# The opening of layer one: norm of tile 1 ahead of tile 2's statistics, tile 2's load ahead of the second weight half, rsqrt steps spread thinner on ScalarE

## Chip, cores, metric

One core of a Trainium2 chip. The metric is the device time of one execution in microseconds (us), lower is better. "Span" is the profile's first to last instruction of one profiled execution; in the runs that have both it is some 1.7 us shorter than the time (1301.6 and 1303.29 for the kernel before). A "slow run" is one in the upper tail of its kernel's runs.

## The reference

Two layers, each a local dilated attention (A) and an MLP over tokens (B), all with a layer norm ahead; 2048 tokens, width 1024, 32 heads, bf16.

```python
x = A_x
x = x + _A_ref(_layernorm(x, axis=-1), A_wqkv, A_wo)   # the change lies in the first microseconds of this line
x = x + _B_ref(_layernorm(x, axis=-1), B_w1, B_b1, B_w2, B_b2)
x = x + _A_ref(_layernorm(x, axis=-1), A_wqkv, A_wo)
x = x + _B_ref(_layernorm(x, axis=-1), B_w1, B_b1, B_w2, B_b2)
```

What matters: the first thing to do is a layer norm of x (16 tiles of 128 tokens) and the V projection of it (two column halves `n` per tile, so 32 units of eight matmuls of 128x512).

## The kernel before

`start_up` writes the instruction order of each engine by hand. For tile `k`: `S_` are two half statistics on VectorE, `A_` aggregates them to mean and variance, `R_` is the rsqrt (a Ln and an Exp on ScalarE), `N_` the norm on VectorE. Tiles 0 to 4 are transposed on TensorE (`tr`) and copied by ScalarE to `hT` in two halves (`C_`); tiles 5 to 15 go through a DMA transpose (`T_`). `V_(k, n, ..)` are the matmuls of one unit, `E_(k, n)` evicts its PSUM tile `m` (two buffers) on ScalarE. `x_load` and `w_load` are loads, all issued by SyncE.

```python
wm = m_tile()
for _ in range(14):                      # dummy matmuls, called "warm" in the profile
    chain_("PE", lambda: nc.tensor.matmul(wm[:], lhsT=warm[:, 0:P], rhs=warm[:], start=True, stop=True))
# ... cut
chain_("SP", x_load, 0, halves)
chain_("SP", x_load, 1)
chain_("SP", w_load, 0, 0)
chain_("SP", w_load, 0, 1)
chain_("SP", x_load, 2)
chain_("SP", x_load, 3)
chain_("SP", w_load, 1, 0)
chain_("SP", w_load, 1, 1)
for k in range(4, NT):
    chain_("SP", x_load, k)
# ... cut
pe = [(tr, 0), (V_, 0, 0, lo4), (tr, 1), (V_, 0, 0, hi4), (V_, 1, 0, lo4), (tr, 2), (V_, 1, 0, hi4),
      (V_, 2, 0, a8), (V_, 0, 1, a8), (tr, 3), (V_, 1, 1, a8), (V_, 2, 1, a8), (tr, 4)]
pe += [(V_, k, n, a8) for k in range(3, NT) for n in range(NDC)]
act = [(R_, 0), (C_, 0), (R_, 1), (C_, 1), (R_, 2), (E_, 0, 0), (C_, 2), (R_, 3), (E_, 1, 0), (R_, 4),
       (E_, 2, 0), (C_, 3), (E_, 0, 1), (R_, 5), (E_, 1, 1), (R_, 6), (C_, 4), (E_, 2, 1), (R_, 7)]
es = [(E_, k, n) for k in range(3, NT) for n in range(NDC)]
for j, e in enumerate(es):
    act.append(e)
    if j + 8 < NT:
        act.append((R_, j + 8))
dve = [(S_, 0, 0), (S_, 0, 1), (A_, 0)]
for k in range(NT):
    nx = k + 1 < NT
    if nx:
        dve.append((S_, k + 1, 0))
    dve.append((N_, k, halves if k == 0 else whole))
    if nx:
        dve += [(S_, k + 1, 1), (A_, k + 1)]
```

The softmax here doesn't subtract the row's maximum and nothing guards it: scores larger than these inputs give would overflow.

## Time and profile before

| | before |
|---|---|
| time, median of 3 (range) | 1304.42 us (1303.2 to 1306.94) |
| span of the profiled execution | 1301.6 us |
| TensorE busy | 98% |
| transposes of tiles 0, 1, 2 start | 6.18, 10.44, 13.23 us |
| unit (3,0) starts | 22.44 us |
| evictions of `m`, 26 to 40 us | 1.99 us apart |

The page of the kernel before; the last line is the chain of work that ended last, by engine.

```profile
span 1301.6 us, 20885 instructions
...
PE 1279.8 (98%) x9240; PEld 581.9 (45%) x9398; DVE 392.8 (30%) x654; ACT 385.1 (30%) x628; POOL 1.7 (0%) x11
...
PE 94%; DVE 3%; issue 1%; ACT 1%; DMA 0%; SPq 0%; another core or an unknown queue 0%
```

TensorE bounds the kernel nearly throughout, so a change of the opening can win only what TensorE loses there. Its timeline (start us, duration us, engine, line, operation, output<-input, count, and in brackets the idle time before and what ended it):

```profile
6.18 0.71 PE L244 MATMUL s<-ident,x 128*128 128x128 bf16 x8
7.57 1.04 PE L257 MATMUL m<-wv,hT 128*128 128x512 bf16 x4 [0.68 <-ACT hT L250]
10.44 0.62 PE L244 MATMUL s<-ident,x 128*128 128x128 bf16 x8 [1.84 <-DVE x L188]
10.90 1.89 PE L257 MATMUL m<-wv,hT 128*128 128x512 bf16 x8
13.23 0.62 PE L244 MATMUL s<-ident,x 128*128 128x128 bf16 x8 [0.45 <-DVE x L188]
13.91 4.26 PE L257 MATMUL m<-wv,hT 128*128 128x512 bf16 x19
...
22.44 39.74 PE L257 MATMUL m<-wv,hT 128*128 128x512 bf16 x173
...
68.70 7.07 PE L351 MATMUL m<-hT,wqk 128*128 128x512 bf16 x32
```

There is one gap of about 2 us ahead of tile 1's transposes (10.44) and a smaller one ahead of tile 2's (13.23); from 13.9 to 22.4 us no further one shows. (The last line, the first q/k matmul, is from a later window.) The chain of waits of the first 15 us (start us, us, what) tells where the first gap comes from:

```profile
3.21 6.00 DMA x<-in_A_x_dram
...
9.24 0.04 DVE bn L226
...
9.85 0.54 DVE x L188
...
10.44 0.63 PE s L244 x8
```

Tile 2's load is issued at 3.21 and lands at 9.2. VectorE waits for it, does the first half of tile 2's statistics, and only then the norm of tile 1 (9.85), which TensorE needs. VectorE's own timeline has the wait, 1.96 us:

```profile
9.24 0.69 DVE L226 BATCH_NORM_STATS2 bn<-x 128x6 f32<-128x512 bf16 x1 [1.96 <-DMA x<-in_A_x_dram]
9.85 0.53 DVE L188 TENSOR_SCALAR x<-x,mv,rs 128x1024 bf16<-128x1024 bf16 x1
```

Tile 1's own scale was there at 8.43.

ScalarE's timeline between 26 and 44 us shows the second loss:

```profile
26.09 0.29 ACT L174 ACTIVATE ln<-mv,eps 128x1 f32<-128x1 f32 x1 [0.98 <-DVE mv L230]
26.42 0.20 ACT L175 ACTIVATE rs<-ln 128x1 f32<-128x1 f32 x1
26.53 0.57 ACT L263 CAST v<-m 128x512 bf16<-128x512 f32 x1
...
28.52 0.57 ACT L263 CAST v<-m 128x512 bf16<-128x512 f32 x1
...
43.00 0.59 ACT L263 CAST v<-m 128x512 bf16<-128x512 f32 x1 [1.40 <-PE m L257]
44.73 0.59 ACT L263 CAST v<-m 128x512 bf16<-128x512 f32 x1 [1.14 <-PE m L257]
```

Every eviction (CAST `v<-m`) stands behind a Ln/Exp pair, which waits about 0.98 us for VectorE's mean and variance, so evictions come at VectorE's 1.99 us, not at TensorE's 1.73 (43.00 to 44.73). TensorE has two `m` buffers and is slowed down to that.

### The profile page before, as it was taken

To read this page: it belongs to the slowest core of one execution; us is meant where nothing else is said; L and a number is where in the kernel's file an instruction comes from. 1 tells how busy PE (TensorE), PEld (TensorE's weight loads), DVE (VectorE), ACT (ScalarE), POOL (GpSimd) and SP (SyncE) were. 2 spreads that over 40 slices of the span, in tenths; PEclk is the share of its full clock that TensorE was granted. 3 is DMA by queue.
4 is the path that set the end of the run, shared out by engine and by line. 5 is a ranking of instruction groups with operands and counts; after the bars stand their busy time and mean duration, and the time that the engine had idled before them with its cause. 6 is when DMAs were issued, how large, how long until landed. Compare 5 with 4: busy or idle time off the path is not lost.

```text
span 1301.6 us, 20885 instructions
## 1 busy us (share of the span) xinstructions
PE 1279.8 (98%) x9240; PEld 581.9 (45%) x9398; DVE 392.8 (30%) x654; ACT 385.1 (30%) x628; POOL 1.7 (0%) x11
## 2 busy tenths in 40 slices
PE   8999999999999999999999999999999999999998
PEld 3444444444444444444444444444444444444443
DVE  7346667820000013232300566688000000111111
ACT  5356776531111110000023667765211111000000
POOL 0000000000000000000000000000000000000000
PEclk9999999999999999999999999999999999999999
DMA  7621113452222236455532100144422222334320
GB/s 235 129 66 34 35 34 98 148 153 82 81 65 84 65 88 159 120 151 152 130 81 57 42 19 19 34 136 156 138 65 81 81 59 76 106 105 136 115 91 33
DMA packets 195818, 121.69 MB, mean 93 GB/s; under 512 B 37904, under 2 KB 177424, under 8 KB 195728
## 3 DMA queue, kind: packets, MB, share of 16 engines
q1 hardware_dynamic: 195728, 120.36, 32.5%
q8 instruction: 73, 1.20, 0.4%
q14 instruction: 17, 0.14, 0.0%
HBM read 96.48 MB, written 16.78 MB: 87 GB/s over the span
## 4 chain that ended last, share of the span: by engine, by line
PE 94%; DVE 3%; issue 1%; ACT 1%; DMA 0%; SPq 0%; another core or an unknown queue 0%
PE m L351 17%; PE s L514 15%; PE s L471 15%; PE acc L471 7%; PE m L471 7%; PE m L514 7%; PE acc L514 7%; PE m L444 7%; PE m L336 4%; PE m L257 2%; PE acc L405 1%; PE s L377 1%; PE acc L409 1%; DVE xn L446 1%; DVE x L188 0%
## 5 line engine op out<-in xcount | busy, mean ns | idle before, releaser
L514 PEld LDWEIGHTS <-w 128*128 128x128 bf16 x1792 | 175.3, 98 | 211.4
L471 PEld LDWEIGHTS <-w 128*128 128x128 bf16 x1792 | 175.3, 98 | 211.4
L351 PE MATMUL m<-hT,wqk 128*128 128x512 bf16 x963 | 231.0, 380 | 7.9 <-issue 7.0
L471 PE MATMUL s<-h,w 128*128 128x512 bf16 x878 | 201.2, 379 | 0.8
L514 PE MATMUL s<-g,w 128*128 128x512 bf16 x884 | 199.3, 379 | 0.7
L517 DVE SCALAR_TENSOR_TENSOR xo<-s,b_sb,xs 128x512 bf16<-128x512 f32 x32 | 24.0, 750 | 540.7 <-PE s L514 530.2
L351 PEld LDWEIGHTS <-wqk 128*128 128x128 bf16 x1024 | 90.5, 98 | 108.7 <-issue 12.9
L386 DVE TENSOR_TENSOR Pm<-pc,band 64x1152 bf16<-64x1152 bf16 x128 | 96.3, 752 | 65.2 <-ACT pc L381 63.2
L444 PE MATMUL m<-wo,oT 128*128 128x512 bf16 x498 | 111.5, 379 | 0.9
L381 ACT ACTIVATE pc<-s,shift 128x576 bf16<-128x576 f32 x128 | 87.8, 737 | 59.9 <-PE s L377 59.9
L471 PE MATMUL acc<-h,w 128*128 128x512 bf16 x440 | 103.1, 379 | 0.5
L514 PE MATMUL acc<-g,w 128*128 128x512 bf16 x436 | 99.7, 379 | 0.5
L471 PE MATMUL m<-h,w 128*128 128x512 bf16 x438 | 98.5, 379 | 0.5
L514 PE MATMUL m<-g,w 128*128 128x512 bf16 x436 | 98.3, 379 | 0.6
L174 ACT ACTIVATE ln<-mv,eps 128x1 f32<-128x1 f32 x64 | 18.9, 296 | 234.5 <-DVE mv L182 222.2
L478 ACT ACTIVATE g<-s,b_sb 128x1024 bf16<-128x1024 f32 x28 | 31.2, 1114 | 166.9 <-PE s L471 155.2
L444 PEld LDWEIGHTS <-oT 128*128 128x128 bf16 x512 | 49.4, 98 | 59.7 <-issue 1.3
L257 PE MATMUL m<-wv,hT 128*128 128x512 bf16 x250 | 56.6, 379 | 1.5 <-ACT hT L250 0.7
L423 DVE TENSOR_TENSOR oT<-acc,rd 128x512 bf16<-128x512 f32 x64 | 44.0, 687 | 39.6 <-ACT rd L421 39.6
L336 PE MATMUL m<-wv,hT 128*128 128x512 bf16 x251 | 55.2, 379 | 0.3
L446 DVE TENSOR_TENSOR xn<-m,xr 128x512 bf16<-128x512 f32 x64 | 44.0, 687 | 8.0 <-PE m L444 6.6
L357 DVE CAST qT<-m 128x512 bf16<-128x512 f32 x32 | 21.8, 681 | 80.8 <-PE m L351 80.8
(59 smaller groups left out, 627.0 us busy)
## 6 DMA issues: line engine op xcount, KB each, us to landing
w<-in_B_w_dram SPq DMA_DIRECT2D x56, 512.0 KB, 3.8
w<-in_B_w_dram SPq DMA_DIRECT2D x64, 448.0 KB, 4.6
wqk<-in_A_wqkv_dram SPq DMA_DIRECT2D x16, 512.0 KB, 5.9
xa<-xn SPq DMA_DIRECT2D x32, 256.0 KB, 2.0
xs<-xa SPq DMA_DIRECT2D x32, 256.0 KB, 3.2
wv<-in_A_wqkv_dram SPq DMA_DIRECT2D x8, 512.0 KB, 5.3
wo<-in_A_wo_dram SPq DMA_DIRECT2D x8, 512.0 KB, 5.0
xr<-in_A_x_dram SPq DMA_DIRECT2D x16, 256.0 KB, 2.9
```

The lines of the kernel that those rows point to most:

```text
L257: r = nc.tensor.matmul(pss_[k, n][:], lhsT=hT[:, kt, cols(*order[k])], rhs=wv[n][kt // 4][:, kt % 4, :], start=(kt == 0), stop=(kt == KD - 1))
L336: nc.tensor.matmul(ps[:], lhsT=hT[:, kt, cols(c, i)], rhs=wv[n][kt // 4][:, kt % 4, :], start=(kt == 0), stop=(kt == KD - 1))
L351: mm = nc.tensor.matmul(ps[:], lhsT=wts[part][:, kt, (g % 2) * P:(g % 2 + 1) * P], rhs=hT[:, kt, lo:lo + 512], start=(kt == 0), stop=(kt = ...
L381: nc.scalar.activation(out=pc[:, 2 * n:2 * n + 2].rearrange("p h t k -> p h (t k)"), in_=ss[n][:, :, 0:HB * HW], func=ACT.Exp, scale=scale ...
L386: nc.vector.tensor_tensor(out=pm[rp, :, b * HB:(b + 1) * HB, r * HK:r * HK + HW], in0=pc[rp], in1=mk, op=ALU.mult)
L423: nc.vector.tensor_tensor(out=oT[g][:, lo:lo + hb * P], in0=acc[:, 0, :], in1=rd[:], op=ALU.mult)
L444: mm = nc.tensor.matmul(ps[:], lhsT=oT[g][:, cols(c, i)], rhs=wo[n][g // 4][:, g % 4, :], start=(g == 0), stop=(g == NG - 1))
L446: nc.vector.tensor_tensor(out=xn[:, xs_], in0=ps[:], in1=xr[:, xs_], op=ALU.add)
L471: nc.tensor.matmul(pairs[fl][0][dc], lhsT=wt[c][:, i, fl * P:(fl + 1) * P], rhs=h2[c][i][:, dc * 512:(dc + 1) * 512], start=(k == 0), stop ...
L478: nc.scalar.activation(out=g[fb][:, fl, :].rearrange("p (n d) -> p n d", n=2), in_=t[:], func=ACT.Gelu_apprx_tanh, bias=b1_sb[:, ft:ft + 1])
L514: nc.tensor.matmul(aps[dc], lhsT=w2t[ft // HF][:, ft % HF, c::DIL], rhs=g[ft // GF][:, ft % GF, dc * 512:(dc + 1) * 512], start=(ft == 0), ...
L517: nc.vector.scalar_tensor_tensor(out=xo[:, dc * 512:(dc + 1) * 512], in0=aps[dc], scalar=b2_sb[:, i, c:c + 1], in1=xs[:, dc * 512:(dc + 1) ...
```

## The change

The intent: take away both losses by order alone. Tile 1's norm goes ahead of tile 2's statistics, tile 2's load ahead of the second weight half, rsqrt 1 between the two copies of tile 0, and the later rsqrt steps go three to four evictions instead of one to one. ScalarE's order for tiles 2 to 6 moves a little as well.

```diff
-        def C_(k):
-            for hf in range(2):
-                ks = slice(hf * KD // 2, (hf + 1) * KD // 2)
-                r = nc.scalar.copy(out=hT[:, ks, cols(*order[k])], in_=tps[k][:, ks, :])
-            return r
+        def C_(k, hf):
+            ks = slice(hf * KD // 2, (hf + 1) * KD // 2)
+            return nc.scalar.copy(out=hT[:, ks, cols(*order[k])], in_=tps[k][:, ks, :])
@@
         chain_("SP", w_load, 0, 0)
+        chain_("SP", x_load, 2)
         chain_("SP", w_load, 0, 1)
-        chain_("SP", x_load, 2)
         chain_("SP", x_load, 3)
@@
-        act = [(R_, 0), (C_, 0), (R_, 1), (C_, 1), (R_, 2), (E_, 0, 0), (C_, 2), (R_, 3), (E_, 1, 0), (R_, 4),
-               (E_, 2, 0), (C_, 3), (E_, 0, 1), (R_, 5), (E_, 1, 1), (R_, 6), (C_, 4), (E_, 2, 1), (R_, 7)]
+        act = [(R_, 0), (C_, 0, 0), (R_, 1), (C_, 0, 1), (C_, 1, 0), (C_, 1, 1), (R_, 2), (E_, 0, 0), (C_, 2, 0), (C_, 2, 1),
+               (E_, 1, 0), (R_, 3), (E_, 2, 0), (R_, 4), (E_, 0, 1), (C_, 3, 0), (C_, 3, 1), (R_, 5), (E_, 1, 1), (R_, 6),
+               (E_, 2, 1), (C_, 4, 0), (C_, 4, 1)]
         es = [(E_, k, n) for k in range(3, NT) for n in range(NDC)]
+        rs = [(R_, k) for k in range(7, NT)]
         for j, e in enumerate(es):
             act.append(e)
-            if j + 8 < NT:
-                act.append((R_, j + 8))
-        dve = [(S_, 0, 0), (S_, 0, 1), (A_, 0)]
-        for k in range(NT):
+            if rs and j % 4 != 3:
+                act.append(rs.pop(0))
+        dve = [(S_, 0, 0), (S_, 0, 1), (A_, 0), (S_, 1, 0), (N_, 0, halves), (S_, 1, 1), (A_, 1), (N_, 1, whole),
+               (S_, 2, 0), (S_, 2, 1), (A_, 2)]
+        for k in range(2, NT):
... (the norm's line in this loop, and the bookkeeping of what must be built before what: cut)
```

More of the change, by code (lines that the diff above doesn't have):

```diff
@@ L301, in start_up @@
                 dve.append((S_, k + 1, 0))
-            dve.append((N_, k, halves if k == 0 else whole))
+            dve.append((N_, k, whole))
             if nx:
@@ L308, in start_up @@
         qs = {"PE": pe, "ACT": act, "DVE": dve, "SP": sp}
-        need = {cast_biases: lambda: (load_biases,) in done, R_: lambda k: k in mvs, N_: lambda k, h: k in rss, tr: lambda k: (N_, k) in done, C_: lambda k: k in tps,
-                V_: lambda k, n, kts: ((C_, k) in done or (T_, k) in done), E_: lambda k, n: (V_, k, n) in done,
+        need = {cast_biases: lambda: (load_biases,) in done, R_: lambda k: k in mvs, N_: lambda k, h: k in rss, tr: lambda k: (N_, k) in done, C_: lambda k, hf: k in tps,
+                V_: lambda k, n, kts: ((C_, k, 1 if kts[-1] == KD - 1 else 0) in done or (T_, k) in done), E_: lambda k, n: (V_, k, n) in done,
                 T_: lambda k: (N_, k) in done}
@@ L321, in start_up @@
                     else:
-                        done.add((f, *args[:1]))
+                        done.add((f, *(args if f is C_ else args[:1])))
     def load_wv():
```

## The prediction

> **What bounds the kernel.** The page shows TensorE busy 98% of 1301.6 us and 94% of the chain that ended last. The change touches only the opening of layer one, so it can win back only TensorE time lost in the first 42 us. The V projection there is 32 units of eight matmuls; one takes 1.727 us where nothing holds it (spacing of the ScalarE evictions of `m` after 43 us, timeline). Everything later just shifts.
>
> **Where TensorE loses now.** (1) Its timeline shows gaps before the transposes of tiles 1 and 2 at 10.44 and 13.23 us. By the chain of waits, tile 1's norm (9.85) stands on VectorE behind the first half of tile 2's statistics (9.24), which waited 1.96 us for tile 2's load, issued at 3.21 behind both 512 KB weight halves, landing 6.0 us later. Tile 1's scale was ready at 8.43, itself behind both copies of tile 0 on ScalarE. (2) From 22 to 40.5 us each eviction stands behind an rsqrt pair that waits about 0.99 us for VectorE's mean/variance: evictions come every 1.99 us instead of 1.727. Unit (3,0) starts at 22.44; freely run, the 11th unit from there would end at 22.44 + 11 x 1.727 = 41.43 and be evicted at 41.6. It was evicted at 43.00: 1.4 us lost (two `m` buffers absorb the rest).
>
> **What the change does.** No work is added or removed; order changes.
> - Norm 1 goes ahead of tile 2's statistics, rsqrt 1 between tile 0's copies. First copy ends about 7.4; rsqrt to 7.95, norm (0.55 us) to 8.5, transpose of tile 1 at 8.55 instead of 10.44.
> - Tile 2's load jumps one 512 KB half. Landings, from the DMA view: about 6.6 (first half), 8.5 (second), 9.2 (tile 2), 10.1 (tile 3). The Trainium skill (DMA: Bandwidth & Descriptors, Queues, rings and completion order) says descriptors on each engine are consumed in ring order; these landings agree. So tile 2 lands at 7.4, the second half at 9.2, used at 9.05: a 0.2 us wait, hidden.
> - Tile 2: statistics 8.45 to 10.0; ScalarE ends tile 1's copies at 10.15; rsqrt to 10.7; norm 10.75 to 11.3; transpose 11.35 instead of 13.23: **1.9 us earlier**. From there TensorE has the same work in the same order (no gap from 13.9 to 22.4), so unit (3,0) starts near 20.6.
> - Three rsqrt pairs per four evictions: 3 x 1.99 = 5.97 us of VectorE loop against 4 x 1.727 = 6.91 us of TensorE, so evictions fall back to TensorE's pace: **1.4 us**. Rsqrts end later, but each DMA transpose (3.1 us to landing) still comes several microseconds ahead of its use.
>
> Both lie fully on the critical path and add: about 3.2 us, 0.25%. Nothing later should give it back: the q/k weights are loaded some 20 us ahead of use.
>
> **Prediction.** 1304.4 - 3.2 = 1301.2 us; range 1299.4 to 1303.2 (the runs of before spread 3.7 us). Faster by over 2%: 0.01; within 2%: 0.98; slower: 0.01.
>
> **What would show it.** Timeline: transpose of tile 1 near 8.6, of tile 2 near 11.4, no 1.96 us wait of VectorE on a load; evictions 1.73 us apart from tile 3 on; first q/k matmul near 65.4 instead of 68.7.
>
> **What would make it wrong.** Tile 4's load (about 13.9) or the second weight pair (13.3) becoming the next wait: slack about 1 us. The second weight half landing well past 9.2. A DMA transpose meeting the x loads, which fill the DMA queue to 20 us. The gain is near the spread between runs.

## The result, and the profile after

| | before | after |
|---|---|---|
| time, median of 6 (range) | 1304.5 us (1303.17 to 1306.94) | 1300.38 us (1299.92 to 1300.72) |
| ratio, 95% interval | | 0.9967 (0.9955 to 0.998) |
| span of the profiled execution | 1301.6 us | 1298.5 us |

Ratios here are the mean time of one kernel's runs over that of the other's of the same rounds, so not quite the ratio of the medians that the text quotes. At the size that can be had here the kernel is faster, and the interval is clear of 1. The six runs of after lie within 0.8 us of each other, those of before within 3.8. That was not predicted and is followed up below.

The page of the kernel after, the lines that answer to those of before:

```profile
span 1298.5 us, 20885 instructions
...
PE 1279.1 (99%) x9240; PEld 582.0 (45%) x9398; DVE 392.9 (30%) x654; ACT 386.0 (30%) x628; POOL 1.7 (0%) x11
...
PE 96%; DVE 2%; issue 1%; ACT 0%; DMA 0%; SPq 0%; another core or an unknown queue 0%
```

TensorE's busy time (1279.8 and 1279.1 us) and the instruction count are as before; the span is 3.1 us shorter, which is TensorE waiting less. TensorE's timeline after:

```profile
6.39 0.72 PE L244 MATMUL s<-ident,x 128*128 128x128 bf16 x8
7.79 1.04 PE L255 MATMUL m<-wv,hT 128*128 128x512 bf16 x4 [0.68 <-ACT hT L249]
8.80 0.62 PE L244 MATMUL s<-ident,x 128*128 128x128 bf16 x8
...
11.60 0.62 PE L244 MATMUL s<-ident,x 128*128 128x128 bf16 x8 [0.33 <-DVE x L188]
...
16.37 0.61 PE L244 MATMUL s<-ident,x 128*128 128x128 bf16 x8
...
20.72 45.06 PE L255 MATMUL m<-wv,hT 128*128 128x512 bf16 x203
65.61 6.64 PE L352 MATMUL m<-hT,wqk 128*128 128x512 bf16 x30
```

The transposes of tile 1 come at 8.80 instead of 10.44, those of tile 2 at 11.60 instead of 13.23, unit (3,0) at 20.72 instead of 22.44. The first q/k matmul is at 65.61; in before's timeline it is at 68.70. VectorE's timeline shows why:

```profile
8.20 0.55 DVE L188 TENSOR_SCALAR x<-x,mv,rs 128x1024 bf16<-128x1024 bf16 x1 [0.70 <-ACT rs L175]
8.66 1.28 DVE L226 BATCH_NORM_STATS2 bn<-x 128x6 f32<-128x512 bf16 x2
...
13.73 0.69 DVE L226 BATCH_NORM_STATS2 bn<-x 128x6 f32<-128x512 bf16 x1 [1.34 <-DMA x<-in_A_x_dram]
14.34 0.53 DVE L188 TENSOR_SCALAR x<-x,mv,rs 128x1024 bf16<-128x1024 bf16 x1
```

The norm of tile 1 now waits only for its own rsqrt (0.70 us), and tile 2's statistics follow without a wait for the load. The wait for tile 4's load that the prediction feared is there (13.73, 1.34 us), but tile 3's norm ends at 14.9, ahead of TensorE's use at 16.37. ScalarE between 26 and 35 us:

```profile
26.10 0.59 ACT L261 CAST v<-m 128x512 bf16<-128x512 f32 x1 [0.45 <-PE m L255]
27.11 0.29 ACT L174 ACTIVATE ln<-mv,eps 128x1 f32<-128x1 f32 x1 [0.43 <-DVE mv L230]
...
27.82 0.59 ACT L261 CAST v<-m 128x512 bf16<-128x512 f32 x1 [0.18 <-PE m L255]
29.55 0.59 ACT L261 CAST v<-m 128x512 bf16<-128x512 f32 x1 [1.14 <-PE m L255]
```

Evictions now come 1.73 us apart and wait for TensorE (`PE m`), no longer the other way round.

### The profile page after: what moved, and what is told of

The parts are those of the page before. It is cut to its first block, busy times and chain, and to the rows that moved or that the text cites. A ratio compares the mean times of both kernels' runs of the same rounds, so it can differ in the third digit from the quotient of the medians.

```text
span 1298.5 us, 20885 instructions
## 1 busy us (share of the span) xinstructions
PE 1279.1 (99%) x9240; PEld 582.0 (45%) x9398; DVE 392.9 (30%) x654; ACT 386.0 (30%) x628; POOL 1.7 (0%) x11
## 4 chain that ended last, share of the span: by engine, by line
PE 96%; DVE 2%; issue 1%; ACT 0%; DMA 0%; SPq 0%; another core or an unknown queue 0%
PE m L352 17%; PE s L515 15%; PE s L472 15%; PE acc L472 7%; PE m L472 7%; PE m L515 7%; PE acc L515 7%; PE m L445 7%; PE m L337 4%; PE m L255 4%; PE acc L406 1%; PE s L378 1%; PE acc L410 1%; DVE xn L447 1%; DVE bn L180 0%
## 5 line engine op out<-in xcount | busy, mean ns | idle before, releaser
L180 DVE BATCH_NORM_STATS2 bn<-xn 128x6 f32<-128x512 bf16 x64 | 44.4, 693 | 1.4
```

Of the source, the lines that this page charges most:

```text
L180: nc.vector.bn_stats(out=s[:, cc, :], in_=x[:, cc * 512:(cc + 1) * 512])
```

## The experiments

In each, the profile marks of TensorE are read from its timeline. A table of them comes first, since it answers most questions. The columns are: start of the transposes of tile 0, of tile 2, of unit (3,0), of the first q/k matmul; then the three stretches between them; then the times of the timed runs. Each experiment ran beside the kernel before on its chip; the median of before in its batch is in the last column.

| run | tile 0 | tile 2 | (3,0) | q/k | 0 to 2 | 2 to (3,0) | (3,0) to q/k | median (range), us | before |
|---|---|---|---|---|---|---|---|---|---|
| before | 6.18 | 13.23 | 22.44 | 68.70 | 7.05 | 9.21 | 46.26 | 1304.5 (1303.17 to 1306.94) | |
| after | 6.39 | 11.60 | 20.72 | 65.61 | 5.21 | 9.12 | 44.89 | 1300.38 (1299.92 to 1300.72) | 1304.5 |
| e1_thin_only | 6.48 | 14.15 | 24.15 | 69.13 | 7.67 | 10.00 | 44.98 | 1302.35 (1302.28 to 1303.71) | 1303.53 |
| e2_open_only | 5.79 | 11.44 | 20.56 | 66.50 | 5.65 | 9.12 | 45.94 | 1301.08 (1301.03 to 1301.78) | 1303.53 |
| e4_load_only | 7.31 | 12.89 | 22.10 | 68.35 | 5.58 | 9.21 | 46.25 | 1302.35 (1302.0 to 1302.94) | 1303.53 |
| e5_norm_only | 7.00 | 12.58 | 21.79 | 68.05 | 5.58 | 9.21 | 46.26 | 1302.63 (1301.92 to 1302.74) | 1303.53 |
| e0_after_again | 6.77 | 11.87 | 20.99 | 65.88 | 5.10 | 9.12 | 44.89 | 1300.46 (1300.37 to 1301.01) | 1303.72 |
| e8_fill | 5.99 | 13.27 | 22.48 | 68.72 | 7.28 | 9.21 | 46.24 | 1303.33 (1303.07 to 1303.88) | 1303.72 |
| e7_further | 5.61 | 11.63 | 20.75 | 65.65 | 6.02 | 9.12 | 44.90 | 1300.03 (1299.86 to 1300.23) | 1303.72 |
| e9_further10 | 5.62 | 11.56 | 20.68 | 65.57 | 5.94 | 9.12 | 44.89 | 1300.19 (1299.88 to 1300.5) | 1303.72 |
| e3_after_old_load | 6.94 | 12.03 | 21.15 | 66.05 | 5.09 | 9.12 | 44.90 | 1300.92 (1300.62 to 1301.74) | 1303.45 |
| e6_no_split | 6.29 | 11.87 | 20.99 | 65.88 | 5.58 | 9.12 | 44.89 | 1300.7 (1300.46 to 1301.55) | 1303.45 |
| e10_late_load | 6.44 | 15.55 | 24.74 | 71.00 | 9.11 | 9.19 | 46.26 | 1305.59 (1304.41 to 1307.55) | 1303.45 |
| e11_late_fill | 6.04 | 14.48 | 23.68 | 69.93 | 8.44 | 9.20 | 46.25 | 1304.65 (1304.53 to 1305.66) | 1303.45 |

(The start of tile 0 varies with the dummy matmuls ahead of it, see e4, and with the landing of tile 1's load, behind whose first statistics tile 0's norm stands in all but e7 and e9.)

### The two halves of the change, each alone

**e1_thin_only**: kernel before, only the late rsqrt steps spread.

```diff
+        rs = [(R_, k) for k in range(8, NT)]
         for j, e in enumerate(es):
             act.append(e)
-            if j + 8 < NT:
-                act.append((R_, j + 8))
+            if rs and j % 4 != 3:
+                act.append(rs.pop(0))
```

> Kernel before with only the rsqrt steps of tiles 8 to 15 spread three to four evictions; opening and loads as before. My theory (two losses, each on TensorE's critical path): the opening keeps its gaps, transpose of tile 2 near 13.2 and of tile 4 near 22.0, but the evictions fall to 1.73 us from about 31 us on, first q/k matmul near 67.3 to 67.4 instead of 68.7 (gain 1.3 to 1.4 us). Rival (once the opening is loose the spreading is worth nothing, the whole 3.1 us of the profile comes from the opening): evictions stay near 1.99 or the gain is under 0.4 us. On the spread between runs: the kernel before spread 3.8 us over six runs, after only 0.8; if that comes from the opening's wait on tile 2's load, this kernel spreads like before (2 us or more).

The last stretch fell from 46.26 to 44.98 us: 1.28 us won there, as expected; the rival is out. But the first q/k matmul came at 69.13, not at 67.3, in this profiled execution, the slowest of the five (1303.71). There are two causes, both in its first 20 us. Tile 2's load landed at 9.88 instead of 9.22 (chain of waits). And the granted clock fell. The busy time by stretch of this run (stretch, its length, then busy us and counts by engine as the first line names them, granted clock, DMA share, GB/s):

```profile
core 0: us, PE busy (x) PEld busy (x) DVE busy (x) ACT busy (x) POOL busy (x), PEclk, DMA share, GB/s
...
10.00:15.00 5.00, 3.90 (x24) 2.21 (x25) 4.08 (x9) 1.94 (x5) 0.00 (x0) 0.74 1.07 376
15.00:20.00 5.00, 5.00 (x28) 2.35 (x27) 3.35 (x8) 2.91 (x8) 0.00 (x0) 0.92 1.05 387
```

and the weight loads of TensorE (PEld in its timeline), with 0.43 us from one to the next (12.87 to 13.30) and idle time put down to "issue", where a full-speed run has 0.22 us:

```profile
12.39 0.20 PEld L257 LDWEIGHTS <-hT 128*128 128x128 bf16 x2 [0.31 <-ACT hT L250]
12.87 0.15 PEld L257 LDWEIGHTS <-hT 128*128 128x128 bf16 x1 [0.28 <-issue]
13.30 0.15 PEld L257 LDWEIGHTS <-hT 128*128 128x128 bf16 x1 [0.28 <-issue]
```

In before's profiled execution the clock is 1.00 in the same stretches. (The clock column also reads 1.00 in the first 5 us of every run, where the weight loads of the dummy matmuls are 0.43 us apart: it shows falls, not the low clock at the start, which is read from the spacing here.) What the fall cost: from tile 1's transposes to unit (3,0) e1 took 13.05 us (11.10 to 24.15) and before 12.00 (10.44 to 22.44), 1.05 us more. So 69.13 is before's 68.70, plus 0.66 for the landing, plus 1.05 for the clock, minus the 1.28 won. The fastest three runs of e1 lie at 1302.28 to 1302.35, two at 1303.54 and 1303.71: a spread of 1.4 us, where 2 or more were expected. The opening is that of before, instruction for instruction, so the slow runs of before may have the same cause. That is a new theory, tested below.

**e2_open_only**: kernel after, the rsqrt steps back behind every eviction.

```diff
-               (E_, 2, 1), (C_, 4, 0), (C_, 4, 1)]
+               (E_, 2, 1), (C_, 4, 0), (C_, 4, 1), (R_, 7)]
-        rs = [(R_, k) for k in range(7, NT)]
+        rs = [(R_, k) for k in range(8, NT)]
-            if rs and j % 4 != 3:
+            if rs:
```

> Kernel after with the rsqrt steps of tiles 7 to 15 put back one behind every eviction; opening as after. My theory: transpose of tile 2 near 11.6, unit (3,0) near 20.7 as in after, then evictions 1.99 us apart again. The rsqrt loop itself starts some 2 us earlier than in before, so the first q/k matmul comes at 66.5 to 66.9: gain over before 1.8 to 2.2 us, so the two parts alone sum to a little more than the 3.1 us of both. Rival (spreading is worth nothing): q/k near 65.6 as after. Spread between runs narrow as in after (under 1.2 us) if the wait on tile 2's load makes the spread.

Unit (3,0) at 20.56, evictions 1.99 us apart again (24.33, 26.32, 28.31), first q/k matmul at 66.50: as expected. Against before of the same rounds the medians fell by 2.45 us here and by 1.18 for e1, together 3.6, a little more than the 3.3 us of the whole change in e0 below; the fastest runs fell by 2.0 and 0.8, against 2.9. (The expected gain for e2 was 1.8 to 2.2: the marks give 2.2, the medians more.) So the two losses are separate, both were on the critical path, and the sum holds within the spread of the runs.

### The pieces of the opening

**e4_load_only** and **e5_norm_only**: kernel before, with only tile 2's load moved up, and with only VectorE's order changed.

```diff
         chain_("SP", w_load, 0, 0)
+        chain_("SP", x_load, 2)
         chain_("SP", w_load, 0, 1)
-        chain_("SP", x_load, 2)
```

```diff
-        dve = [(S_, 0, 0), (S_, 0, 1), (A_, 0)]
-        for k in range(NT):
+        dve = [(S_, 0, 0), (S_, 0, 1), (A_, 0), (S_, 1, 0), (N_, 0, halves), (S_, 1, 1), (A_, 1), (N_, 1, whole),
+               (S_, 2, 0), (S_, 2, 1), (A_, 2)]
+        for k in range(2, NT):
```

> Kernel before with only tile 2's load put ahead of the second weight half. My theory: the load lands near 7.9 instead of 9.2, VectorE's order no longer blocks norm 1: norm 1 near 8.5, transpose of tile 1 near 9.1, of tile 2 near 11.9 (1.3 to 1.4 us earlier than before), all kept to the first q/k matmul, near 67.3. So this one line alone would give most of the opening's gain. Rival (the norm order is what counts, a load order that changes nothing in its consumer's order does little): under 0.4 us. Spread between runs: narrow if the wait on the load makes the spread.

> Kernel before with only VectorE's order changed (norm 1 and all statistics of tile 2 as in after); loads and ScalarE as before. My theory: norm 1 near 8.5, transpose of tile 1 near 9.1; tile 2's statistics still wait for its load at 9.2, end near 10.7, transpose of tile 2 near 12.0: 1.2 to 1.3 us earlier, first q/k matmul near 67.4. So norm order and load order each alone win most of it: they take away the same wait and overlap. Rival (their gains add): this one and the load alone sum to the 1.6 us by which after advances tile 2's transpose, so at least one of them is under 0.9 us.

The marks of the profiled executions missed by 0.6 to 1.0 us (tile 2's transposes at 12.89 and 12.58 instead of near 12). The reason is a thing that neither theory had: in these two executions the clock rose late, so nearly all of the 14 dummy matmuls ran at 0.43 us each and TensorE came to tile 0 only at 7.31 and 7.00. The stretch from there to tile 2 (5.58 us in both) does not compare cleanly with before's 7.05, because before waits for a load that lands at a fixed time, however early or late tile 0 was. So the times must judge: the medians fell by 1.18 and 0.9 us, the fastest runs by 1.04 and 1.12. Each alone wins about 1 us, a little under the 1.2 to 1.4 expected, and the rival "a load order does little" is out. Whether the two gains overlap these two cannot say: 0.9 is just the rival's bound. The next run can.

**e3_after_old_load**: kernel after with the load order of before (the first of the two diffs above, undone).

```diff
         chain_("SP", w_load, 0, 0)
-        chain_("SP", x_load, 2)
         chain_("SP", w_load, 0, 1)
+        chain_("SP", x_load, 2)
```

> Kernel after with tile 2's load back behind the second weight half. The load alone and the norm order alone each moved the time by 0.9 to 1.2 us in the medians, both of them with the rsqrt split by 2.5. My theory: they take away the same wait, so undoing one costs little: tile 2 lands near 9.3 instead of 7.9, its statistics start then instead of 8.7, its transposes 0.3 to 0.5 us later than in after, time 0.2 to 0.7 us over after's 1300.4. Rival (their gains add): 1.0 us or more over after. TensorE has no gap over 1.5 us, so no slow tail: five runs within 1.2 us.

Median 1300.92, 0.46 us above e0's. The two ran on different chips, so each against its own before: the medians fell by 2.53 us here and by 3.26 in e0, the fastest runs by 2.46 and 2.91. By these figures the load order is worth 0.45 to 0.7 us where the norm order is in place and about 1.1 alone: the gains overlap by about half. They speak against the rival's 1.0 us or more; the intervals of the two ratios (0.9968 to 0.9993 here, 0.9961 to 0.9986 in e0) are too wide to exclude it. In the profiled execution tile 0 started late (6.94), tile 1's norm with it (8.64), and tile 2's statistics followed at 9.10 without any wait for the load: there the late load did no harm at all. Two of the five runs are about 1 us above the fastest (1301.58 and 1301.74).

**e6_no_split**: kernel after with rsqrt 1 behind both copies of tile 0.

```diff
-        act = [(R_, 0), (C_, 0, 0), (R_, 1), (C_, 0, 1), (C_, 1, 0), (C_, 1, 1), (R_, 2), ...
+        act = [(R_, 0), (C_, 0, 0), (C_, 0, 1), (R_, 1), (C_, 1, 0), (C_, 1, 1), (R_, 2), ...
```

> Kernel after with rsqrt 1 behind both copies of tile 0 again. My theory: rsqrt 1 is now what norm 1 waits for, so it ends 0.45 to 0.5 us later, transpose of tile 1 near 9.3 and of tile 2 near 12.0; time 0.3 to 0.6 us over after's 1300.4. Rival (slack elsewhere takes it up): within 0.15 us of after. No slow tail.

Tile 0 to tile 2 took 5.58 us, 0.37 to 0.48 longer than after's: the split is worth what was expected in that stretch. In time, the medians of before and this kernel differ by 2.75 us, against 3.26 in e0, so 0.5 us; the fastest runs by 2.62 against 2.91. That is about what was expected, though the bare medians of this kernel and e0, on different chips, are only 0.24 us apart. One run (1301.55) is 1.1 us above the fastest; like e3's 1301.58 it has a granted clock of 1.000, so not every late run comes from the clock.

### The spread between runs: a fall of the clock

**e0_after_again**: the kernel after, unchanged, on the chip of the next three.

> Kernel after unchanged, on the chip of the next runs. It fixes the yardstick: both theories expect a median 3.0 to 4.2 us under before's. Theory of the clock (found in the profile of the spreading-alone run: TensorE idle for 2.2 us before tile 2's statistics are done, weight loads then 0.43 us apart instead of 0.22 between 12.9 and 15.8 us): after has no such long gap, so its runs stay within 1.2 us of one another while before's spread 2.5 us or more, and the difference of the fastest runs is 3.0 to 3.4 us while that of the medians is as large or larger.

Ratio 0.9973 (0.9961 to 0.9986). Medians differ by 3.26 us, the fastest runs by 2.9, just under the 3.0 expected. The spread of before in this batch was 1.8 us, not 2.5; after's was 0.64. Counting all four batches, 12 of 33 runs of before are above 1304.2 us, more than 1 us over its fastest (1303.04); of the 11 of after none is more than 1.1 us over its fastest.

**e8_fill**: kernel before plus eight dummy matmuls in the gap.

```diff
+        def W_(n):
+            for _ in range(n):
+                r = nc.tensor.matmul(wm[:], lhsT=warm[:, 0:P], rhs=warm[:], start=True, stop=True)
+            return r
-        pe = [(tr, 0), (V_, 0, 0, lo4), (tr, 1), ...
+        pe = [(tr, 0), (V_, 0, 0, lo4), (W_, 8), (tr, 1), ...
```

> Kernel before plus eight further dummy matmuls behind tile 0's first four value matmuls, 8 x 0.216 = 1.7 us in the 1.84 us gap ahead of tile 1's transposes; nothing else. Theory of the clock: TensorE no longer idles there, so it never falls back to the low clock; the fastest run stays within 0.4 us of before's fastest, but the slow tail of before (over 1.5 us above its fastest) goes: all five runs within 1.2 us, median 0.3 to 0.8 us under before's. Rival (the tail comes from the landing time of tile 2's load, which this kernel waits for just as before): the tail stays, spread 2 us or more, median as before's.

Five runs between 1303.07 and 1303.88, where four of before's nine lie between 1304.67 and 1305.06; median 0.39 us lower. It still waits for tile 2's load (9.28 on VectorE), which speaks against the landing time alone as the tail. It is weak evidence by itself: with 12 slow runs of 33, five clean ones come by luck about one time in ten ((21/33) to the fifth power).

**e10_late_load** and **e11_late_fill**: the gap made longer on purpose, unfilled and filled.

```diff
+        chain_("SP", w_load, 1, 0)
         chain_("SP", x_load, 2)
         chain_("SP", x_load, 3)
-        chain_("SP", w_load, 1, 0)
```

(e10's edit; e11 has it too, and 15 dummy matmuls in the place where e8 has eight.)

> Kernel before with the loads of tiles 2 and 3 put behind one more 512 KB weight half: the suspected wait is made longer on purpose. Tile 2 lands 1.5 to 1.7 us later (near 10.8), transpose of tile 1 near 12.0, TensorE idle some 3.2 us ahead of it. Without any effect of the clock that shifts all by 1.5 to 1.7 us: 1304.8 to 1305.2. Theory of the clock: the idle time now brings TensorE back to the low clock in most or all runs, weight loads 0.43 us apart after the gap, costing 1 to 2 us more: median 1305.8 to 1307.2. Rival (no clock effect, or a rare one): median near 1305.0.

> The same late loads, with the gap filled by 15 dummy matmuls (15 x 0.216 = 3.2 us). Theory of the clock: the same late landing, but no fall of the clock: 1304.7 to 1305.3, all runs within 1.2 us; the difference from the unfilled one is what the clock costs, 1 to 2 us. Rival: same as the unfilled one within 0.4 us.

The unfilled one ran 1304.41 to 1307.55, the filled one 1304.53 to 1305.66; medians 0.94 us apart, means 1.0 (1305.92 and 1304.90). The expected 1 to 2 us is at best just reached, the expected median of the unfilled one missed by 0.2, and its fastest runs (1304.41 and 1304.94) have a granted clock of 1.000, so even a gap of 3 us does not bring a fall every time. Busy time from 10 to 15 us of the unfilled one (e10):

```profile
core 0: us, PE busy (x) PEld busy (x) DVE busy (x) ACT busy (x) POOL busy (x), PEclk, DMA share, GB/s
...
10.00:15.00 5.00, 3.01 (x14) 1.69 (x15) 2.91 (x6) 1.70 (x5) 0.00 (x0) 0.66 1.06 378
```

and of the filled one (e11):

```profile
core 0: us, PE busy (x) PEld busy (x) DVE busy (x) ACT busy (x) POOL busy (x), PEclk, DMA share, GB/s
...
10.00:15.00 5.00, 4.50 (x32) 2.19 (x32) 3.63 (x7) 1.94 (x5) 0.00 (x0) 1.00 1.06 380
```

The granted clock from 10 to 15 us is 0.66 without and 1.00 with the dummy matmuls. In steps of 1 us the clock column of e10 reads 0.71, 0.50, 0.50, 0.58 from 11 to 15 us, and that of e1 0.69, 0.50, 0.50, 0.60 from 12 to 16: taken as time at 0.50, that is 0.58 + 1 + 1 + 0.84 and 0.62 + 1 + 1 + 0.80, 3.4 us in both. So reckoned, the fall begins near 11.4 in e10, inside the gap, and near 12.4 in e1, 1.3 us after TensorE had resumed (11.10). In e10 the weight loads are 0.43 us apart from 12.7 to 14.9 us. The fall is not all of the difference between the two profiled executions (1305.59 and 1304.53): from tile 1's transposes to unit (3,0) e10 took 12.75 us and e11 12.00, so 0.75 is the clock, and another 0.31 is tile 2's load, which landed later in e10 (10.79 and 10.48 on VectorE).

Only one execution of each kernel was profiled, but the record has the mean granted clock, to three decimals, of every run told here except before's first six:

| kernels | longest gap of TensorE in the opening (profiled), us | runs | clock below 1.000 | 0.998 or lower |
|---|---|---|---|---|
| before | 1.84 | 27 | 12 | 6 |
| e1 | 2.18 | 5 | 3 | 0 |
| e10 | 3.11 | 5 | 3 | 2 |
| e8, e11 (before's gap, filled) | 0.68 | 10 | 1 | 0 |
| after, e0, e2 to e7, e9 | 0.75 | 46 | 2 | 0 |

All eight of these runs of before above 1304.2 us are among its twelve below 1.000. A reading of 0.999 is not always this fall: in the profiled executions of e2 and e11 the clock is 1.00 throughout the opening. So a gap on TensorE in this opening can cost more than itself: in up to half of the runs the clock falls, and where a profile shows it, it cost 0.75 (e10) and 1.05 us (e1).

### Going further

**e7_further** and **e9_further10**: kernel after, with tile 0's norm ahead of tile 1's statistics, rsqrt 2 between the copies of tile 1, and 12 or 10 dummy matmuls.

```diff
-... (A_, 0), (S_, 1, 0), (N_, 0, halves), (S_, 1, 1), ...
+... (A_, 0), (N_, 0, halves), (S_, 1, 0), (S_, 1, 1), ...
-... (C_, 1, 0), (C_, 1, 1), (R_, 2), ...
+... (C_, 1, 0), (R_, 2), (C_, 1, 1), ...
-        for _ in range(14):
+        for _ in range(12):          # 10 in e9_further10
```

> Kernel after, further: tile 0's norm ahead of tile 1's statistics, rsqrt 2 between the two copies of tile 1, 12 instead of 14 dummy matmuls. Norm 0 near 5.1 instead of 5.9, transpose of tile 0 at 5.6 to 6.5 (the dummy matmuls' end sets it when the clock rises late), first value matmuls wait for the first weight half at about 7.2, transpose of tile 1 near 8.3 instead of 8.8, of tile 2 near 11.0 instead of 11.6; first q/k matmul 65.0 to 65.2; time 0.4 to 0.6 us under after's. Rival (what TensorE waits for here is the second weight half at about 9.3, so nothing is won): within 0.2 us of after.

> As the further kernel, with 10 dummy matmuls: they end by 1.38 + 10 x 0.427 = 5.65 us at the low clock, so they never hold tile 0's transposes. If the clock rises as it did so far [...], the same or 0.1 to 0.3 us faster than with 12, with less spread; rival: the clock rises later or falls again because TensorE is busy for a shorter time, the first value matmuls run 0.43 us apart, and runs are 0.5 us or more slower in the median or in a tail.

Both beat after in the median on the same chip: 1300.03 and 1300.19 against 1300.46. The ranges of e7 (1299.86 to 1300.23) and e0 (1300.37 to 1301.01) do not meet; those of e9 (up to 1300.5) and e0 do. Part of the rival is right too: TensorE now stops for the second weight half. Its timeline in e9:

```profile
8.50 0.62 PE L244 MATMUL s<-ident,x 128*128 128x128 bf16 x8
9.69 1.89 PE L255 MATMUL m<-wv,hT 128*128 128x512 bf16 x8 [0.56 <-DMA wv<-in_A_wqkv_dram]
11.56 0.62 PE L244 MATMUL s<-ident,x 128*128 128x128 bf16 x8
```

Tile 0 started at 5.6 us as expected, but tile 2 at 11.6 instead of near 11.0: what was gained ahead is waited for at 9.69, and from there TensorE runs on without a stop. The change's own opening has this wait too when tile 0 is early: 0.75 us at 9.57 in e2, where tile 0 began at 5.79. In e7 TensorE stops for 0.62 us at the same place (9.75); the trace names a copy of ScalarE there, but the first matmuls to stop need only tile 0's copies, done at 8.35, and the second weight half landed at about 9.7 (3.21 + 6.5, DMA view). With 10 dummy matmuls tile 0's transposes ran at the low clock in this execution (1.06 instead of 0.62 to 0.72 us); no tail came of it. Between 12 and 10 the runs do not decide.

## Why the prediction was right

- **Total.** Predicted 3.2 us less, 1301.2; measured 1300.38, 4.1 us less in the medians of the first batch, 3.3 in the second, 3.1 between the two profiled executions. The sum of the mechanism, 1.9 + 1.4, came out in the profiles as 1.72 (unit (3,0), 22.44 to 20.72) and 1.37 (the stretch from there, 46.26 to 44.89). Of the 1.72, 1.63 is tile 2's transposes; 0.09 comes after them (9.21 to 9.12), in every kernel with after's ScalarE order for tiles 2 to 6 and in none with before's.
- **The opening.** Transposes of tiles 1 and 2 predicted at 8.55 and 11.35, found at 8.80 and 11.60. Both 0.25 late, 0.2 of it for one reason: tile 1's load landed at 5.3 instead of 5.1, and tile 0's norm stands behind tile 1's first statistics (tile 0's transposes at 6.39 instead of 6.18). e7 and e9 took that wait away, and met the second weight half.
- **The loads.** The Trainium skill (DMA: Bandwidth & Descriptors, Queues, rings and completion order) says that each DMA engine consumes descriptors in ring order. The swap agrees: issue and landing by the DMA view gave 7.9 us for tile 2 (2.67 + 5.2) and 9.3 for the second half (3.21 + 6.1), where before tile 2 took 6.0 us from 3.21. Predicted were 7.4 and 9.2. TensorE's wait for the second half, 0.2 us and hidden in the prediction, did not show in after, where tile 0 began at 6.39, but was 0.75 us in e2, where it began at 5.79.
- **The order of the pieces.** The prediction counted norm order, load order and split as one gain. e4 and e5 show that load and norm order each win about 1 us alone; by e3 the load order is worth about half of that once the norm order is there, and by e6 the split adds 0.3 to 0.5.
- **The thinner rsqrt steps.** Confirmed alone (e1: 1.28 us) and by undoing (e2: 1.99 us spacing returns).
- **What was missed.** The prediction took the spread of before, 3.8 us, for noise between runs. Part of it is the kernel's own: TensorE's idle gap lets the granted clock fall in some executions (0.74 in e1, 0.66 in e10, 1.00 where filled). By closing the gap the change also removes that tail; this would explain why the medians' 4.1 us in the first batch, with four slow runs of six, exceed the 3.1 us of the profiles. Shown: the fall in the profiles of e1 and e10, its absence in that of e11 with the gap filled, and over all runs a clock below 1.000 in 18 of 37 with the gap and in 3 of 56 without it. Not shown: that the fall is the whole of each slow run. The clocks of before's first six runs are not on record, no run of 0.998 or lower was profiled, and a late landing of tile 2's load (9.88 in e1, 9.22 in before) gives a part as well.

## What to carry to other kernels

An instruction waiting for a late load held up what stood behind it in the engine's written order (1.96 us on VectorE here), so put the work that is ready and wanted ahead of it; moving the load or the consumer does much of the same job, and the second of the two paid only about half of what it pays alone. Where one engine carries both a free-running stream (evictions) and a slower dependent loop (rsqrt), give the loop no more places than it can fill in time (here 1.73 us of TensorE over 1.99 us of loop, at most 0.87 per eviction; three in four fits), so that the loop does not set the pace of the stream. And when a kernel's runs spread by more than its neighbours' do, look at the granted clock after the first gaps of TensorE before calling it noise.

## What the Trainium skill lacked or had wrong

- TensorE: Matmul & The Clock Gate (Part 1 and "Why this matters for your kernels") gives an idle window of about 3.4 us, or gaps over about 3 us, for a fall to half clock. Here the clock fell (0.74 granted from 10 to 15 us) behind an idle gap of 2.2 us (e1, 8.92 to 11.10, the time before it also only partly busy), and in e10 near the end of one of 3.1 us, in some runs and not in others. A gap of 2 us is not safe in this opening.
- The same page advises to warm up with 4 us or more of matmuls before a benchmark, and says that the rise varies from run to run. The variation agrees: weight loads turn from 0.43 to 0.22 us apart between about 4 us (e2) and about 7 us (e4), which is some 2.6 to 5.8 us after the first matmul at 1.38, so 4 us of matmuls did not always do. The page does not say what a fixed number of dummy matmuls costs when the rise is late: in e4 tile 0's norm began at 6.15, so its transposes could have begun near 6.6 (0.46 us behind, as in after), and began, behind the 14 dummies, at 7.31.
- No page that was read says that dummy matmuls in a short gap in mid-kernel can pay: with them e8's five runs spread 0.8 us against 1.8 of before, and e11's median lay 0.94 us under e10's (0.75 of the 1.06 between their profiled executions is the clock).
